# The first steps of a token-mixing kernel: plain products instead of a seven-product scheme, and an earlier start for the rows and weights that feed them

## The chip, the cores and the metric

The kernel runs on one core of one Trainium2 chip. The metric is the device time of one execution in microseconds (us). Three executions of the kernel before took 1442.42, 1442.47 and 1443.08 us; the median is 1442.47 us. Engines are named as in the profile: PE (matrix products), PEld (its weight loads), DVE (vector engine), ACT (scalar engine), POOL and SP (here they mostly issue DMAs). A PSUM tile is the accumulator that PE writes; DVE and ACT read it out.

## The reference

With B = 8 batches, S = 4224 tokens and D = 192 channels, cut to what matters:

```python
# lightweight convolution: 7 taps per head, causal, softmaxed weights
x = einsum('hk,bskhg->bshg', softmax(weight), windows(x))
# phase mixing
theta = x @ w_theta
zr, zi = x * cos(theta), x * sin(theta)
y = einsum('ts,bsd->btd', w_tok_r, zr) + einsum('ts,bsd->btd', w_tok_i, zi)
u = x + y
out = u + relu(u @ w_ch)
```

Nearly all of the arithmetic is the token mixing: two 4224 x 4224 matrices (real and imaginary) applied to 1536 columns (8 batches of 192 channels).

## The kernel before, in words

**Chunks and steps.** The 4224 source tokens are cut into 33 chunks of 128 (class `Chunk`), the 4224 target tokens into 33 blocks of 128, two blocks making a *unit*. At most NW = 11 chunks are held in SBUF. A `Step` mixes all chunks that are held with the weights of one unit and adds the result to the unit's partial rows `pv` (DRAM `part0`/`part1` between steps). In the first steps the chunks are still arriving: step 0 has n = 2 chunks, step 1 has 4, step 2 has 5, step 3 has 7, step 4 has 9, all later ones 11.

**A chunk's preparation** has this order: its rows are loaded by POOL (`xw`, L197) and the 16 rows ahead of them copied from the chunk before by SP (L188); `conv(0)` and `conv(1)` are 8 matmuls each into a PSUM tile `pc` (L210), read out into the chunk's tile `z` (L151 on ACT or L149 on DVE); 12 transposes into `tp` (L165), read out into `uT`; `theta(0)` and `theta(1)` are 8 matmuls each into `v` (L141, one for each half of the batches), each followed by two sines on ACT (L246: cosine and sine); then on DVE two products x·cos and x·sin (`product`, L251) and four differences T1, T2, T3, T4 (`sums`, L257). `pc`, `v` and `tp` share two PSUM buffers, so each of these PE groups also waits until the tile two places before it has been read out.

**A step's weights.** POOL loads the fp32 weights as 16-bit into a staging tile `st` (L323, two buffers, one for the real and one for the imaginary matrix of a step). DVE turns four blocks of them (`turn`, L336: "11" and "21" from the real one, "12" and "22" from the imaginary one) and forms four sums (`wsum`, L348: S1 to S4). A new `st` load can be issued only when the block turned last from the old one is done. POOL and SP issue in a fixed order, so what waits holds up all that stands behind it.

**A step's products** (`runs`, `mix`, L443). Seven products of a Strassen-like scheme stand for the eight that two target blocks (1, 2) and two matrices on two channel halves would need. Each product is a *run* over the step's n chunks (2 matmuls of 128 x 384 per chunk). Runs alternate between two or three PSUM accumulators, and an accumulator is given out to `pv` in the middle of its life and then accumulated further:

```python
("11", Z11, "c1", True, (0, 0, True)),
("S1", T1, "c2", True, (1, 1, True)),
("S2", T2, "c1", False, (0, 1, True)),
("S4", Z22, "c2", False, (0, 1, False)),
("S3", T3, "c1", False, (1, 1, False)),
("12", Z21, "c3", True, (0, 0, False)),
("22", T4, "c1", False, (1, 0, True)),
```

The last column is what is given at the end of the run: target block, channel half, and whether a first visit may copy. `give` (L400 to L408) copies with ACT (L406) where it may, and adds with DVE (L408) where not; in the steps of the first round a step has four copies and three adds. The next run on the same accumulator has to wait for the give. There are two PSUM buffers for accumulators (`ypool`), so the third accumulator "c3" also waits for the give of S4.

**What sets the order.** Every engine's order is the order in which the program is written (`in_order`). The front (L664 to L711) is a loop over i = 0 to 12 that prepares chunk i and finishes chunk i - 1, and calls `more(n)` between the pieces, which takes up to n matmul pairs from the stream of mixing as far as the chunks are ready (`ready[0]`); in the first turns it puts in dummy matmuls instead (`idle`, L590). Work of the next steps (turns, weight sums, loads of weights and rows, `step_events`) hangs on positions 0 to 7 inside a step.

Of the kernel before, what the change touches and what calls it, by code (L numbers as in the profile page):

```python
# [10 lines left out]
ALU = mybir.AluOpType  # L11
# [5 lines left out]
def kernel(  # L17
# [42 lines left out]
    NU = (NT + 1) // 2  # L60
    NW = 11
    PC = 512

    base = [0, 0, 1, 1, 2, 3, 3, 4, 4, 5, 5]
    assert len(base) == NW
# [65 lines left out]
    def token(k, a):  # L131

        return (a * NK + k) * Q
# [39 lines left out]
        )  # L173

    Z11, T1, Z21, Z22, T2, T4, T3 = range(7)

    class Chunk:

# [23 lines left out]
        def conv(self, j):  # L202

            if j == 0:
                self.z = zpool.tile([P, 7, HN], F16, name="z", tag="z")
                self.x = self.z[:, T2 : T2 + 2, :].rearrange("p t n -> p (t n)")
            pc = banks("pc")
            for h in range(4):
                for half in range(2):
                    pe(nc.tensor.matmul(  # L210
                        pc[half * 2 * Q : (half + 1) * 2 * Q, h // 2,
                           h % 2 * B * G : (h % 2 + 1) * B * G],
                        lhsT=bands[:, 4 * j + h, :, :].rearrange("p a m -> p (a m)"),
                        rhs=self.xw[:, half, :, (4 * j + h) * G : (4 * j + h + 1) * G],
                        start=True, stop=True,
                    ))
            evacuate(
                self.x.rearrange("p (b d) -> p b d", d=D)[
                    :, :, 4 * j * G : 4 * (j + 1) * G
                ].rearrange("p b (i h g) -> p i h b g", i=2, h=2),  # L220
                pc[:, :, 0 : 2 * B * G].rearrange("p i (h b g) -> p i h b g", h=2, b=B),
                self.k == 0 and j == 1,
            )
            if j == 1:
                for a in range(NQ):
                    t0 = token(self.k, a)
                    nc.sync.dma_start(
                        out=xs[t0 : t0 + Q, :], in_=self.x[a * Q : (a + 1) * Q, :]
                    )

        def transpose(self):
            self.xT = turned()
            transposed(self.xT, self.x, range(NG), self.k < 2)

        def theta(self, g):
            v = channel_mix(self.xT[:, 6 * g : 6 * g + 6, :], wth).rearrange(
                "p k (b h e) -> p k b h e", b=2, h=2
            )
            for first, bias in ((Z11, half_pi[:]), (Z21, None)):
                o = self.z[:, first : first + 2, :].rearrange(  # L240
                    "p h (k b e) -> p k b h e", b=2, e=HD
                )[:, 2 * g : 2 * g + 2, :, :, :]
                args = dict(out=o, in_=v, func=AT.Sin)
                if bias is not None:
                    args.update(bias=bias, scale=1.0)
                act(nc.scalar.activation(**args))  # L246

        def product(self, first):
            o = self.z[:, first : first + 2, :].rearrange("p h (b e) -> p h b e", e=HD)
            xv = self.x.rearrange("p (b h e) -> p h b e", h=2, e=HD)  # L250
            dve(nc.vector.tensor_tensor(out=o, in0=xv, in1=o, op=ALU.mult))  # L251

        def sums(self, which):
            z = self.z
            for o, a, b in (((T3, Z22, T1), (T1, T1, Z11)),
                            ((T2, Z22, T1), (T4, Z21, T2)))[which]:
                dve(nc.vector.tensor_tensor(  # L257
                    out=z[:, o, :], in0=z[:, a, :], in1=z[:, b, :], op=ALU.subtract
                ))

        def tasks(self):

# [22 lines left out]
    class Step:  # L285


        def __init__(self, t):
            self.t, self.u, self.ks = t, unit(t), active(t)
            self.n = len(self.ks)  # L290
            self.tbs = [tb for tb in (2 * self.u, 2 * self.u + 1) if tb < NT]
            self.pair = len(self.tbs) == 2
            self.first = t < NU
            self.final = t + NU >= NSTEP
            self.late = self.final and self.n < NW
            visits = [v for v in range(NU, NSTEP) if v % NU == t % NU]
            quiet = [v for v in visits if start[2 * NW - 1] < v <= 2 * NU]
            self.adds, self.ahead = [], []
            for i, tb in enumerate(self.tbs):
                known = self.known(tb)  # L300
                if t not in ([v for v in quiet if known < v - 1] or visits[-1:])[:1]:
                    continue
                if not self.late:
                    self.adds.append(i)
                else:
                    far = known <= start[2 * NW - 1]
                    self.ahead.append((i, 2 * NU - NW + 2 * (t % NU) if far else start[-1],
                                       (t // NU - 1 - far) % 2))
            self.time = 0.324 * self.n * (7 if self.pair else 4)
            self.st, self.w, self.xr, self.ub, self.uT, self.pv = {}, {}, {}, {}, {}, []  # L310

        def known(self, tb):
# [41 lines left out]
        def w_tasks(self):  # L354

            if not self.pair:
                return [(0.25, lambda: self.turn("11")), (4.2, lambda: self.turn("12"))]
            return [
                (0.25, lambda: self.turn("11")), (1.2, lambda: self.turn("21")),
                (2.05, lambda: self.wsum("S3")), (2.2, lambda: self.turn("22")),  # L360
                (3.05, lambda: self.wsum("S1")), (3.3, lambda: self.wsum("S2")),
                (4.2, lambda: self.turn("12")), (5.1, lambda: self.wsum("S4")),
            ]
# [46 lines left out]
        def runs(self):  # L410
# [16 lines left out]
                ("12", Z22, "c2", False, (0, 1, False)),  # L427
            ]

        def mix(self, events):  # L430

            runs = self.runs()
            events = sorted(events, key=lambda e: e[0])
            y = {}
            for r, (wn, zn, cn, opens, to) in enumerate(runs):
                if opens:
                    y[cn] = ypool.tile([P, 2, PC], F32, name="y", tag="y")
                for c, k in enumerate(self.ks):
                    while events and events[0][0] * len(runs) <= 7 * (r + c / self.n):
                        events.pop(0)[1]()  # L440
                    yield k
                    for q in range(2):
                        pe(nc.tensor.matmul(  # L443
                            y[cn][:, q, 0:BH],
                            lhsT=self.w[wn][:, c, :, :].rearrange("p bt i -> p (bt i)"),
                            rhs=chunks[k].z[:, zn, q * BH : (q + 1) * BH],
                            start=(opens and c == 0), stop=(c == self.n - 1),
                            skip_group_check=True,
                        ))
                if to:  # L450
                    self.give(y[cn], *to)
            for _, f in events:
# [52 lines left out]
            return found  # L505

    steps = [Step(t) for t in range(NSTEP)]
    outputs = [
        (sum(s.time for s in steps[: t + 1]) + at, f)
        for t in range(NSTEP) if steps[t].final for at, f in steps[t].outputs()  # L510
# [2 lines left out]
    def step_events(t):  # L513
# [11 lines left out]
        if t + 2 < NSTEP:  # L525
            nxt = steps[t + 2]
            for m in (1, 2):
                found.append((1.3 + 3 * (m - 1), lambda m=m: nxt.load_w(m)))
        if t == NU - 2:
            def load_wch():  # L530
                dve(nc.vector.memset(wch[:, 1:3, :], 0.0))
# [129 lines left out]
    load_chunk(3)  # L661
    for m in (1, 2):
        steps[1].load_w(m)
    for i in range(NW + 2):  # L664
        ch = chunks.get(i) if i < NW else None
        old = chunks[i - 1] if 0 < i <= NW else None

        def between(n):
            left = more(n)
            if 0 < i < 3:  # L670
                idle(min(left, 2))

        if ch:
            ch.conv(0)
        between(2)
        if old:
            old.theta(0)
        between(1)
        if ch:
            ch.conv(1)  # L680
        if i == 0:
            idle(4)
        ready[0] = i - 2
        between(2)
        if old:
            old.theta(1)
        if i == 1:
            for at, f in steps[0].w_tasks():
                if at < 2.2:
                    f()  # L690
        if i + 3 < NW:
            load_chunk(i + 3)
        between(1)
        if ch:
            ch.transpose()
        if old:
            old.product(Z11)
        between(2)
        if i == 1:
            for at, f in steps[0].w_tasks():  # L700
                if at >= 2.2:
                    f()
        if old:
            old.product(Z21)
        between(1)
        if old:
            old.sums(0)
        between(1)
        if old:
            old.sums(1)  # L710
        between(1)  # L711
    ready[0] = NK
# [33 lines left out]
```

## Time and profile before

| what | value |
|---|---|
| median of the three executions | 1442.47 us |
| the profiled execution | 1441.24 us |
| its span (first to last instruction) | 1439.4 us |
| PE busy in the span | 1410.6 us, 98% |
| DVE busy | 977.7 us, 68% |
| ACT busy | 316.0 us, 22% |
| POOL busy | 435.2 us, 30% |
| mean of the matmuls of the mixing (L443) | 326 ns from start to end, 7656 of them |

The times of a matmul overlap with the next one's, so a group is costed by starts: 47 matmuls of the mixing take 7.80 us from 92.52 us on, 0.166 us each. Busy shares are a mean over the span; the front has other limits than the rest, so it is read from the waits and the timeline of its own stretch. In rows of the timeline the first two numbers are start and duration, the brackets give the idle time of the engine before the row and what ended it.

### The profile page before, as it was taken

The page shows a single profiled execution, that of the slowest core. Times are in us where ns is not written, and L with a number is a line of the kernel's source. Part 1 is how long each engine was busy: PE and PEld are TensorE (multiplying, and loading weights), DVE is VectorE, ACT ScalarE, POOL GpSimd, SP SyncE. Part 2 cuts the span into 40 slices and gives each one's busy share as a digit, 9 for nine tenths or more (in the row PEclk, how much of TensorE's full clock was granted, in tenths as well). Part 3 has the DMA queues.
Part 4 walks back from the last instruction along what each step waited for, and adds up shares of the span by engine and source line. Part 5 has one row for each costly group of instructions (what it writes and reads, how often), then busy time and mean ns, then how long its engine had stood idle before and what let it go on. Part 6 is the DMA issues. An engine that isn't in the chain of part 4 may idle for free.

```text
span 1439.4 us, 23742 instructions
## 1 busy us (share of the span) xinstructions
PE 1410.6 (98%) x9809; PEld 890.2 (62%) x9809; DVE 977.7 (68%) x1050; ACT 316.0 (22%) x379; POOL 435.2 (30%) x655
## 2 busy tenths in 40 slices
PE   7899999999999999999999999999999999999997
PEld 4556666666666666666666666666566666666665
DVE  6893555545548787766666657877777677767686
ACT  6861101111125254000000004435200110010133
POOL 8421211111233232532433343233323123213120
PEclk9999999999999999999999999999999999999999
DMA  9976756465699999998899989989999999999884
GB/s 174 244 159 144 147 102 151 87 150 100 132 234 214 238 247 227 231 243 181 218 253 214 243 143 248 238 188 251 264 219 202 213 213 212 204 204 189 167 207 141
DMA packets 272028, 281.98 MB, mean 196 GB/s; under 512 B 106672, under 2 KB 240176, under 8 KB 271920
## 3 DMA queue, kind: packets, MB, share of 16 engines
q0 software_dynamic: 162464, 92.15, 48.8%
q1 hardware_dynamic: 71824, 178.88, 35.2%
q10 hardware_dynamic: 37632, 9.44, 4.6%
q8 instruction: 77, 1.26, 0.3%
q14 instruction: 31, 0.25, 0.1%
HBM read 245.49 MB, written 108.13 MB: 246 GB/s over the span
## 4 chain that ended last, share of the span: by engine, by line
PE 89%; DVE 4%; DMA 2%; ACT 2%; issue 1%; POOL 1%; DVEq 0%; SPq 0%; ACTq 0%
PE y L443 81%; PE v L141 5%; PE tp L165 1%; DMA xw<-in_x_dram 1%; PE pc L210 1%; ACT z L246 1%; DMA xw<-xw 1%; DVE pv L408 1%; DVE z L257 1%; DVE z L251 1%; DVE wt L336 1%; POOL st L323 0%; DVE pv L476 0%; ACT uT L151 0%; DVE wt L348 0%
## 5 line engine op out<-in xcount | busy, mean ns | idle before, releaser
L443 PE MATMUL y<-z,wt 128*128 128x384 f16 x7656 | 1279.6, 326 | 10.0 <-DVE pv L408 6.9
L443 PEld LDWEIGHTS <-wt 128*128 128x128 f16 x7656 | 742.5, 98 | 487.3 <-issue 9.8
L408 DVE TENSOR_TENSOR pv<-y,pv 128x768 f32<-128x768 f32 x324 | 309.1, 954 | 321.1 <-PE y L443 281.0
L336 DVE STREAM_TRANSPOSE wt<-st 128x1408 f16<-128x1408 f16 (+7 forms) x224 | 327.9, 1466 | 45.4 <-PE y L443 39.1
L323 POOL DMA_DIRECT2D st<-in_moe_w_tok_r_dram x232 | 132.7, 579 | 459.5 <-DVE wt L336 455.9
L323 POOL DMA_DIRECT2D st<-in_moe_w_tok_i_dram x232 | 132.7, 579 | 410.4 <-DVE wt L336 402.8
L348 DVE TENSOR_TENSOR wt<-wt 128x1408 f16<-128x1408 f16 (+7 forms) x216 | 174.4, 807 | 41.2 <-PE y L443 38.5
L151 ACT ACTIVATE z<-pc 128x768 f16<-128x768 f32 x65 | 50.9, 818 | 386.0 <-PE pc L210 383.3
L151 ACT ACTIVATE ub<-pv 128x768 f16<-128x768 f32 x63 | 50.3, 837 | 334.2 <-DVE pv L408 311.7
L406 ACT ACTIVATE pv<-y 128x768 f32<-128x768 f32 x66 | 54.1, 819 | 281.6 <-PE y L443 281.6
L141 PEld LDWEIGHTS <-uT 128*128 128x128 f16 x1056 | 91.2, 98 | 26.2 <-issue 7.8
L386 POOL TENSOR_TENSOR pv<-pv,xr 128x1536 f32<-128x1536 f32 x24 | 74.5, 3104 | 63.9 <-DVE pv L476 21.9
L197 POOL DMA_DIRECT2D xw<-in_x_dram x132 | 76.3, 585 | 28.2 <-DMA xw<-xw 8.3
L476 DVE SCALAR_TENSOR_TENSOR pv<-v,pv 128x768 f32<-128x768 f32 x66 | 62.9, 955 | 27.5 <-PE v L141 27.0
L257 DVE TENSOR_TENSOR z<-z 128x768 f16<-128x768 f16 x132 | 73.4, 556 | 3.6
L151 ACT ACTIVATE uT<-tp 128x1536 f16<-128x1536 f16 (+1 forms) x49 | 59.8, 1222 | 56.5 <-PE tp L165 56.5
L246 ACT ACTIVATE z<-v,half_pi 128x768 f16<-128x768 f32 x66 | 59.9, 908 | 55.0 <-PE v L141 54.4
L251 DVE TENSOR_TENSOR z<-z 128x1536 f16<-128x1536 f16 x66 | 60.0, 948 | 6.6 <-ACT z L246 6.6
L141 PE MATMUL v<-wth,uT 128*128 128x192 f16 x528 | 55.0, 248 | 4.8 <-ACT z L246 2.8
L141 PE MATMUL v<-wch,uT 128*128 128x192 f16 x528 | 54.2, 246 | 2.1 <-DVE pv L476 1.2
L246 ACT ACTIVATE z<-v 128x768 f16<-128x768 f32 x66 | 53.5, 811 | 0.0
L210 PE MATMUL pc<-xw,bands 96*64 96x192 f16 x528 | 31.4, 255 | 1.4 <-DVE bands L630 0.8
(43 smaller groups left out, 141.5 us busy)
## 6 DMA issues: line engine op xcount, KB each, us to landing
part<-pv SPq DMA_DIRECT2D x79, 768.0 KB, 4.2
pv<-part SPq DMA_DIRECT2D x79, 768.0 KB, 6.1
out_dram<-pv SPq DMA_DIRECT2D x66, 384.0 KB, 4.5
st<-in_moe_w_tok_r_dram POOLq DMA_DIRECT2D x136, 176.0 KB, 5.9
st<-in_moe_w_tok_i_dram POOLq DMA_DIRECT2D x136, 176.0 KB, 5.1
xs<-z SPq DMA_DIRECT2D x132, 96.0 KB, 4.9
xw<-in_x_dram POOLq DMA_DIRECT2D x121, 96.0 KB, 5.5
xr<-xs SPq DMA_DIRECT2D x24, 384.0 KB, 4.6
```

Of the source, the lines that this page charges most:

```text
L141: pe(nc.tensor.matmul(v[:, k, b * D : (b + 1) * D], lhsT=tT[:, 3 * k + b + i, :], rhs=w[:, 2 * b + i, :], start=(i == 0), stop=(i == 1),))
L151: act(nc.scalar.activation(out=out, in_=in_, func=AT.Copy))
L197: nc.gpsimd.dma_start(out=self.xw[lo : lo + n, h, :, :], in_=x[:, t0 : t0 + n, :].rearrange("b s d -> s b d"),)
L246: act(nc.scalar.activation(**args))
L251: dve(nc.vector.tensor_tensor(out=o, in0=xv, in1=o, op=ALU.mult))
L257: dve(nc.vector.tensor_tensor(out=z[:, o, :], in0=z[:, a, :], in1=z[:, b, :], op=ALU.subtract))
L323: pool(nc.gpsimd.dma_start(out=st[a * Q : (a + 1) * Q, 0:nb, :, 0:n] .rearrange("i r bt s -> i (r bt) s"), in_=w[self.tbs[0] * P : (self.t ...
L336: dve(nc.vector.transpose(self.w[name][:, 0 : self.n, :, :], self.st[int(name[1])][:, int(name[0]) - 1, :, 0 : self.n * Q] .rearrange("p b ...
L348: dve(nc.vector.tensor_tensor(out=self.w[name][:, 0 : self.n, :, :], in0=self.w[a][:, 0 : self.n, :, :], in1=self.w[b][:, 0 : self.n, :, : ...
L386: ins = pool(nc.gpsimd.tensor_tensor(out=self.pv[i], in0=self.pv[i], in1=self.xr[i], op=ALU.add))
L408: dve(nc.vector.tensor_tensor(out=o, in0=yv, in1=o, op=ALU.add))
L443: pe(nc.tensor.matmul(y[cn][:, q, 0:BH], lhsT=self.w[wn][:, c, :, :].rearrange("p bt i -> p (bt i)"), rhs=chunks[k].z[:, zn, q * BH : (q + ...
```

## The change

- **Plain products.** Where a step of the first round has a pair of target blocks and at most NP = 4 chunks (steps 0 and 1, `plain`), it mixes the eight plain products: four blocks of weights, each with two channel halves, no S and no T operands. Each of the four results is given once, by a copy. The first target block is mixed chunk by chunk, the second one half after the other.
- **Order of the slots.** The second half of x·cos (Z12) is now made in the slot of T3 (`raw`), so that T1 is a new tile and T3 is formed in place. Chunks 0 to 3 need no T operands until step 2; their T1, T2, T4 are formed during step 1 and their T3 during step 2 (`step_events`).
- **Chunk 0 in batch halves.** Its convolution, transposes and products are each made in two halves of four batches (`conv_batches`, `transpose_batches`, `product` with `gs`). It has 32 convolution matmuls of 96 columns instead of 16 of 192.
- **Who reads PSUM out.** DVE instead of ACT takes the transposes of chunks 2 and 3, both convolution halves of chunk 1 and the second ones of chunks 2 and 3; chunk 0 is shared.
- **Rows and turns.** The loads of chunks 4 and 5 are written ahead of the loop. The turns of steps 0 and 1 are written into turns i = 1 and i = 3 of the loop. `ready[0]` is raised one piece sooner. The dummy matmuls fall from 33 to 21.

The built order shows what of this the engines see. On POOL the loads of chunks 4 and 5 stand where they stood, behind both weight loads of step 1; the first weight load of step 3 now stands ahead of chunk 8 instead of behind it. On SP the store of step 0's first `pv` block now stands ahead of the halo copies of chunk 5 instead of behind those of chunk 6. From step 4 on all engines have the order that they had.

```diff
+    NP = 4
+    Z12 = T3
@@ conv
-                self.k == 0 and j == 1,
+                self.k == 1 or (self.k in (2, 3) and j == 1),
@@
+        def conv_batches(self, g):
...
+            for h in range(H):
+                for half in range(2):
+                    pe(nc.tensor.matmul(
+                        pc[half * 2 * Q : (half + 1) * 2 * Q, h // 4,
+                           h % 4 * GB * G : (h % 4 + 1) * GB * G],
+                        lhsT=bands[:, h, :, :].rearrange("p a m -> p (a m)"),
+                        rhs=self.xw[:, half, g * GB : (g + 1) * GB, h * G : (h + 1) * G],
+                        start=True, stop=True,
+                    ))
+            for i in range(2):
+                evacuate(
...
+                    i == 1,
+                )
+        def raw(self, first):
+            return self.z[:, 0:7:6, :] if first == Z11 else self.z[:, Z21 : Z21 + 2, :]
@@ transpose
-            transposed(self.xT, self.x, range(NG), self.k < 2)
+            transposed(self.xT, self.x, range(NG), self.k < 4)
+        def transpose_batches(self, g):
+            if g == 0:
+                self.xT = turned()
+            transposed(self.xT, self.x, [g], True)
@@ sums
-            for o, a, b in (((T3, Z22, T1), (T1, T1, Z11)),
+            for o, a, b in (((T1, Z12, Z11), (T3, Z22, Z12)),
@@ Step
-            self.time = 0.324 * self.n * (7 if self.pair else 4)
+            self.plain = self.first and self.pair and self.n <= NP
+            self.time = 0.324 * self.n * (8 if self.plain else 7 if self.pair else 4)
@@ w_tasks
+            if self.plain:
+                return []
@@
+        def products(self):
...
+            for i, name in enumerate(("c1", "c2")):
+                a, b = f"{i + 1}1", f"{i + 1}2"
+                cells = [
+                    (r, c, h) + w for c in range(self.n) for h in range(2)
+                    for r, w in enumerate(((a, (Z11, Z12)[h]), (b, (Z21, Z22)[h])))
+                ]
+                if i:
+                    cells.sort(key=lambda e: (e[2], e[0]))
+                for r, c, h, wn, zn in cells:
+                    done = r == 1 and c == self.n - 1
+                    yield (wn, zn, f"c{h + 1}", c, r == 0 and c == 0, done,
+                           (i, h, True) if done else None)
@@ step_events
+        if t in (NPS, NPS + 1):
+            for j, k in enumerate(k for k in range(NK) if start[k] <= NPS):
+                for o, a, b, at in (
+                    ((T1, Z12, Z11, 0), (T2, Z22, T1, 0.3), (T4, Z21, T2, 0.6)),
+                    ((T3, Z22, Z12, 0),),
+                )[t - NPS]:
+                    found.append((
+                        (1.3 + 1.4 * j if t == NPS else 1.2 + 0.6 * j) + at,
+                        lambda k=k, o=o, a=a, b=b: chunks[k].sum(o, a, b),
+                    ))
@@ the loop of the front
-    for i in range(NW + 2):
+    load_chunk(4)
+    load_chunk(5)
+    for g in range(NG):
+        chunks[0].conv_batches(g)
+    idle(2)
+    for g in range(NG):
+        chunks[0].transpose_batches(g)
+    for i in range(1, NW + 2):
...
-            if 0 < i < 3:
-                idle(min(left, 2))
+            if i < 3:
+                idle(min(left, 2) if i == 1 else 0)
...
-        if i == 1:
-            for at, f in steps[0].w_tasks():
-                if at < 2.2:
-                    f()
+        if i in (1, 3):
+            for name in ("11", "21"):
+                steps[i // 2].turn(name)
...
+        if i in (1, 3):
+            for name in ("12", "22"):
+                steps[i // 2].turn(name)
...
-        if old:
+        if old and start[i - 1] > NPS:
             old.sums(0)
```

## The prediction

> **What bounds the kernel now.** I read four views, from coarse to fine. The page says that PE is busy 98% of the span; after about 104 us it hardly waits at all, so whatever the change does lies ahead of that, and the time moves with the moment from which PE runs without waits. The waits of PE in the first 100 us name what holds it there:
>
> ```profile
> PE y L443 <- ACT pv L406: 3.0, 3, 1.2
> PE v L141 <- ACT z L246: 2.8, 7, 0.7
> PE y L443 <- DVE pv L408: 2.7, 4, 1.0
> ```
>
> The gives of step 0 (L406, L408) cost about as much as the sines. The timeline of PE shows where:
>
> ```profile
> 33.53 0.81 PE L443 MATMUL y<-z,wt 128*128 128x384 f16 x4 [1.13 <-ACT pv L406]
> 35.57 0.48 PE L443 MATMUL y<-z,wt 128*128 128x384 f16 x2 [1.23 <-ACT pv L406]
> ...
> 37.72 0.82 PE L443 MATMUL y<-z,wt 128*128 128x384 f16 x2 [0.78 <-DVE pv L408]
> 38.33 1.49 PE L141 MATMUL v<-wth,uT 128*128 128x192 f16 x8
> ```
>
> With two chunks a run of step 0 is 4 matmuls, 0.7 us; a give takes 0.8 to 0.95 us, so runs wait for gives, and theta of chunk 3 stands behind them. It also runs in 1.49 us instead of 0.82 us, at a granted clock of 0.71 between 36 and 40 us. Then the timeline of DVE:
>
> ```profile
> 43.68 1.83 DVE L251 TENSOR_TENSOR z<-z 128x1536 f16<-128x1536 f16 x2 [1.48 <-ACT z L246]
> ...
> 50.45 1.83 DVE L251 TENSOR_TENSOR z<-z 128x1536 f16<-128x1536 f16 x2 [1.81 <-ACT z L246]
> ...
> 58.93 0.84 DVE L336 STREAM_TRANSPOSE wt<-st 128x640 f16<-128x640 f16 x1 [1.41 <-PE y L443]
> ...
> 81.34 1.11 DVE L336 STREAM_TRANSPOSE wt<-st 128x896 f16<-128x896 f16 x1 [1.43 <-PE y L443]
> ...
> 102.76 0.95 DVE L408 TENSOR_TENSOR pv<-y,pv 128x768 f32<-128x768 f32 x1
> ```
>
> From chunk 3's first product (43.68) to the add of step 3's run S4 (102.76, ends 103.71) DVE idles 1.81 + 1.41 + 1.43 = 4.65 us of 60.0. Last the chain of waits: from 82.38 us it lies on DVE (products, differences, adds) until
>
> ```profile
> 102.84 0.88 DVE pv L408
> 103.77 6.35 PE y L443 x38
> ```
>
> where PE, which stood for 2.31 us, takes run "12" and never waits long again. So **the time moves with the moment at which DVE ends this add**.
>
> **Step 1: until chunk 3's sines end.** In the built order I lay the instructions end to end with the durations of the rows. Equal until 9.94 us.
> - Chunk 0: 32 convolution matmuls for 16 (1.43 us). A matmul of half the columns is not in the trace; its weight load is (0.072 us), the whole one took 0.089, so 2.3 to 2.85 us, I take 2.6. Its four half readouts at 0.5 and its half transposes follow one another, two dummies go. First theta at 15.4 instead of 15.08: 0.3 us lost; if half a matmul costs half, 0.6 gained.
> - Chunk 1: dummies ahead of it go, theta at 20.8 instead of 21.04.
> - Chunk 2: its transposes are read out by DVE (0.96, end 26.05) instead of ACT (1.45, end 27.35), theta at 26.2 instead of 27.41. DVE is free for it: its turns shrink by the four sums of 0.29.
> - Chunk 3: transposes 29.7; before, uT waited behind two sines and a copy on ACT and began at 33.32; on DVE 30.55 to 31.45. A plain step has no give inside; the fifth matmul pair of block 2 waits only for the second copy (31.8). Convolution of chunk 4 at 32.2 (35.99), theta at 33.3 (38.33) at the full clock, second theta 35.8 (41.83), sines end 38.6. Before, 43.52 + 0.83 = 44.35.
>
> So chunk 3's first product could begin at 38.6 instead of 43.68: **5.1 us**. Chunk 4's rows hide behind this: POOL issues them from 24.75 (25.12 before), since it still waits for step 0's turns; at the row's 4.8 us to landing they are there at 31.9, 0.3 us ahead of need. "Sooner" is worth nothing here, and each us of lateness would cost one.
>
> **Step 2: DVE from there to the add.** Costed by starts: a difference 0.555 (four in 2.22), an add 0.93. In this stretch before, 32 differences and 7 adds. After: chunks 0 to 3 bring T1, T2, T4, T3 here, 44 in all, +12 x 0.555 = 6.7; three adds of step 1 are gone, -2.8. Products (16), turns and weight sums of steps 2 to 4 stay. Work +3.9: 55.4 + 3.9 = 59.3 us. The idle 4.65 us go: two of its gaps were waits for sines, and ACT now runs ahead (its period was 50.97 - 44.21 = 6.8 us per chunk, DVE's work is 59.3 / 8 = 7.4); the other two were turns that waited for a weight tile, and a plain step uses four of the nine tiles instead of eight. **Net gain of the stretch 0.75 us.**
>
> New idle time: the first turn of step 2 stands ahead of chunk 3's product and waits for its weights. POOL issues them when step 1's turns end (30.15) and chunk 4's rows land, 30.4 to 32.7; at 5.0 us they land at 37.7, the turn (0.84) ends at 38.5. That cover is gone if they are later, and two stores of 768 KB from step 0 now leave SP at about 32 and 36.5 instead of 44.45. What lies beside such stores is in the list of DMA issues, for the issues from 44.3 to 47 us (times to landing last):
>
> ```profile
> part<-pv SPq DMA_DIRECT2D x2, 768.0 KB, 7.4
> xw<-in_x_dram POOLq DMA_DIRECT2D x4, 96.0 KB, 9.3
> ```
>
> 9.3 instead of about 4.8. Weights beside a store: 5.0 to 9.3. I take 1.0 us late, nearer to 5.0, since one store, not two, lies beside them. Plus 0.4 us for chunk 10: PE's run "12" of step 2 needs the add of that step's S4. Up to its end DVE has 36.6 us of rows from 38.6, so about 76 with the lateness; PE is there at about 72 and stands some 4 us, and chunks 9 and 10 follow that.
>
> **Step 3: PE and the rest.** Plain products add (4 + 8) matmuls x 0.166 = 2.0 us; 12 dummies go. Neither is on the path: PE would be at run "12" of step 3 by 94.5 (from chunk 4's uT to chunk 10's last theta 44.21 to 92.52 before, so 38.6 + 48.3 = 86.9; then 46 matmuls x 0.166 = 7.6), DVE's add ends at 38.6 + 59.3 + 1.4 = 99.3. From there the order is the same. Sum: -5.1 - 0.75 + 1.0 + 0.4 = **-4.4 us**: 1441.24 becomes 1436.8; for the median of the runs 1442.47 - 4.4 = 1438.1.
>
> The clock: 0.71 was granted after gaps of only 1.13, 1.23 and 0.78 us. The Trainium skill, "TensorE: Matmul & The Clock Gate", Part 1, halves the clock after an idle window of some 3.4 us. No gap here was that long, so the row decides that short gaps do it too; by the page the new stand of 4 us ahead of "12" would halve the clock for up to 3.4 us, an estimate of 1.7 us on PE, of which some 1 us would reach chunk 10's sines and the add. That speaks against the change; by it the sum would be -3.4.
>
> **Rivals.**
> 1. *Loads late, gain eaten.* Step 2's real weights land after 9.3 us, at 42.0; the turn ends at 42.8, chunk 3's product begins 4.2 us later than it could: 4.2 replaces 1.0, gain 1.2, 1441.3. For it: DMA engines are over 90% busy from 4 to 40 us. Against: step 2's weights took 5.0 before.
> 2. *Loads late twice, slower.* The real weights take 10.5 us (the longest of a row load in this trace) and land at 43.2; the imaginary ones are issued only after that load's first parts, at about 41 to 43, and take as long, to 53.7, where DVE wants them at 48.6. That idles DVE 5.4 + 5.1 us, so -5.1 - 0.75 + 10.5 + 0.4 = +5.1: 1447.6. It decides from a sum of 8.3 us of lateness on.
> 3. *DVE is no bound.* If differences and products hide better than by their rows, PE goes on at 94.5 to 95.5 instead of 103.77: 8.3 us less at the later end, 1434.2. Against: the chain lies on DVE already, and its work grows.
> 4. *The first part doesn't come.* Chunk 0 in halves and the rows' place are as good as neutral above; if the gives were not the cause, chunk 3 would stay at 44.35 and only the added 3.9 us against 4.65 would be left: 1441.7. The three named waits speak against it.
>
> **Chances.** Forecast (gain 2.5 to 6.5) 0.62; rival 1: 0.15; rival 2: 0.08; rival 3: 0.08; rival 4: 0.07. Range 1434.0 to 1443.5: it takes in rivals 1, 3 and 4 and leaves rival 2 out. What the measurement can tell from no change is about 0.2%, 2.9 us: faster 0.63 (rival 3 and all of the forecast but 0.07), same 0.29, slower 0.08.
>
> **What would show it.** Right: no wait for L406 or for an add in the first 40 us; chunk 3's first product at 38.5 to 40; DVE without idle gaps from there; PE waiting for the add of S4 in step 2 (3 to 4 us, near 72) and again ahead of "12" in step 3, going on at 99 to 100. Wrong: a turn of 640 columns that waits for a DMA for more than 2 us (rivals 1, 2); DVE gaps of over 2 us in all after 45; PE waiting for rows; or a granted clock under 0.9 for long in the front.

## The result and the profile after

The changed kernel takes 1437.35 us (median of 16 runs, 1435.46 to 1441.31) against 1441.68 us for the kernel before (16 runs, 1439.83 to 1449.47): 4.3 us less, a ratio of 0.9969 with a 95% interval of 0.9960 to 0.9977. Forecast were 4.4 us less. The profiled execution took 1437.24 us with a span of 1435.4 us, 4.0 us under that of before. The page's busy times, then the head of its chain:

```profile
PE 1410.6 (98%) x9825; PEld 890.3 (62%) x9825; DVE 973.8 (68%) x1046; ACT 310.8 (22%) x374; POOL 434.4 (30%) x655
...
PE 90%; DMA 5%; DVE 2%; ACT 1%; POOL 1%; issue 1%; DVEq 0%; ACTq 0%; POOLq 0%; SPq 0%
```

PE is as busy as before; its share of the chain rose from 89% to 90%, DVE's fell from 4% to 2%, and DMA's rose from 2% to 5%. That last pair tells what took over. PE's waits in the first 100 us:

```profile
PE pc L212 <- DMA xw<-xw: 3.3, 3, 1.6
...
PE y L513 <- ACT pv L454: 1.0, 2, 0.7
```

The waits for gives, 3.0 us on ACT and 2.7 us on DVE before, have shrunk to 1.0 us. New is 3.3 us of waiting for halo copies (L190). The timeline of PE has the theta of chunk 3, the new stall and the end of the stretch:

```profile
33.22 0.82 PE L142 MATMUL v<-wth,uT 128*128 128x192 f16 x8
...
71.59 0.24 PE L212 MATMUL pc<-xw,bands 96*64 96x192 f16 x1 [1.61 <-DMA xw<-xw]
72.79 0.82 PE L212 MATMUL pc<-xw,bands 96*64 96x192 f16 x7 [0.96 <-DMA xw<-xw]
...
100.93 7.33 PE L513 MATMUL y<-z,wt 128*128 128x384 f16 x44 [1.83 <-DVE pv L456]
```

Theta of chunk 3 runs 5.1 us sooner, at the full clock (0.82 instead of 1.49 us); run "12" of step 3 goes on at 100.93 instead of 103.77. DVE over the same stretch:

```profile
39.87 0.84 DVE L382 STREAM_TRANSPOSE wt<-st 128x640 f16<-128x640 f16 x1 [5.63 <-DMA st<-in_moe_w_tok_r_dram]
40.64 1.78 DVE L293 TENSOR_TENSOR z<-z 128x1536 f16<-128x1536 f16 x2
...
47.25 0.84 DVE L382 STREAM_TRANSPOSE wt<-st 128x640 f16<-128x640 f16 x1 [2.04 <-DMA st<-in_moe_w_tok_i_dram]
...
87.09 1.83 DVE L293 TENSOR_TENSOR z<-z 128x1536 f16<-128x1536 f16 x2 [1.20 <-ACT z L287]
...
99.92 0.95 DVE L456 TENSOR_TENSOR pv<-y,pv 128x768 f32<-128x768 f32 x1
```

Chunk 3's sines end at 37.74 + 0.84 = 38.58, and yet its product begins at 40.64, because the turn ahead of it waits for step 2's weights. The second load costs 2.04 us, chunk 9's sines 1.20 us. Where these come from is in the chain of waits:

```profile
58.06 1.10 POOL xw L199 x2
59.18 8.02 DMA xw<-in_x_dram
67.32 5.33 DMA xw<-xw
72.79 0.82 PE pc L212 x7
```

Chunk 9's rows take 8.0 us and its halo copy is issued behind SP's two stores of step 1 (768 KB each, issued from 58.30); PE gets it at 72.8, and what follows runs at half speed: the granted clock from 72.6 to 76.0 is 0.50. So theta of chunk 9 and its sines are late.

**Where the 4.0 us of span lie.** I take one turn of DVE, the one that starts at 205.75 us in the changed kernel, as a mark; counted from the end it is the same instruction in every kernel here, and from well ahead of it on PE, DVE and ACT have the same order. Before reaches it at 208.59: 2.84 us lie ahead of the mark, the other 1.1 us behind it, in code that the change doesn't touch. How far that second part differs from one execution to another, the column "rest" of the table below shows.

### The profile page after: what moved, and what is told of

The parts are those of the page before. It is cut to its first block, busy times and chain, and to the rows that moved or that the text cites. A ratio compares the mean times of both kernels' runs of the same rounds, so it can differ in the third digit from the quotient of the medians.

```text
span 1435.4 us, 23761 instructions
## 1 busy us (share of the span) xinstructions
PE 1410.6 (98%) x9825; PEld 890.3 (62%) x9825; DVE 973.8 (68%) x1046; ACT 310.8 (22%) x374; POOL 434.4 (30%) x655
## 4 chain that ended last, share of the span: by engine, by line
PE 90%; DMA 5%; DVE 2%; ACT 1%; POOL 1%; issue 1%; DVEq 0%; ACTq 0%; POOLq 0%; SPq 0%
PE y L513 81%; PE v L142 5%; DMA xw<-in_x_dram 2%; DMA st<-in_moe_w_tok_r_dram 2%; PE tp L166 1%; PE pc L212 1%; ACT z L287 1%; DVE wt L382 1%; POOL st L369 1%; DVE pv L456 1%; DVE pv L546 0%; POOL xw L199 0%; DMA xw<-xw 0%; DMA st<-in_moe_w_tok_i_dram 0%; DMA wsb<-in_weight_dram 0%
## 5 line engine op out<-in xcount | busy, mean ns | idle before, releaser
L456 DVE TENSOR_TENSOR pv<-y,pv 128x768 f32<-128x768 f32 x318 | 303.3, 954 | 321.4 <-PE y L513 281.3
L382 DVE STREAM_TRANSPOSE wt<-st 128x1408 f16<-128x1408 f16 (+7 forms) x224 | 327.4, 1465 | 50.1 <-PE y L513 36.2
L394 DVE TENSOR_TENSOR wt<-wt 128x1408 f16<-128x1408 f16 (+6 forms) x208 | 173.3, 833 | 40.2 <-PE y L513 38.0
L152 ACT ACTIVATE z<-pc 128x768 f16<-128x768 f32 (+1 forms) x62 | 47.5, 803 | 385.6 <-PE pc L212 381.3
L152 ACT ACTIVATE uT<-tp 128x1536 f16<-128x1536 f16 (+1 forms) x47 | 56.7, 1209 | 56.9 <-PE tp L166 56.9
L293 DVE TENSOR_TENSOR z<-z 128x1536 f16<-128x1536 f16 (+1 forms) x68 | 60.6, 926 | 4.2 <-ACT z L287 4.2
```

Of the source, the lines that this page charges most:

```text
L152: act(nc.scalar.activation(out=out, in_=in_, func=AT.Copy))
L382: dve(nc.vector.transpose(self.w[name][:, 0 : self.n, :, :], self.st[int(name[1])][:, int(name[0]) - 1, :, 0 : self.n * Q] .rearrange("p b ...
L394: dve(nc.vector.tensor_tensor(out=self.w[name][:, 0 : self.n, :, :], in0=self.w[a][:, 0 : self.n, :, :], in1=self.w[b][:, 0 : self.n, :, : ...
L456: dve(nc.vector.tensor_tensor(out=o, in0=yv, in1=o, op=ALU.add))
```

## The experiments

My theory was that plain products let chunk 3 finish sooner, and that from there DVE, fed by the weight loads, sets the moment at which PE runs free. Rivals: the readouts that moved to DVE, or chunk 0's halves, make the gain; PE is the bound; the loads set it all. Each kernel ran 10 to 12 times. "Ratio" is to runs of the kernel before, taken beside it. The table is worked out from the traces: the first convolution matmul, the mark at 205.75 us less that start (the front), the span behind the mark (the rest), and the start of the add behind S4 of step 3, counted from the start of the span, so that the five kernels with a first convolution at 8.9 us have 1.1 us of advance in it. A trace shows one execution, which took up to 3.8 us more (e1) or 2.5 us less (e2) than the median of its kernel, so front and rest do not add up to the median.

```
kernel                first conv   front   rest    S4 add   median   ratio (95%)
before                    9.94    198.65  1230.8   102.76   1441.68  1
changed                   9.96    195.79  1229.7    99.92   1437.35  0.9969 (0.9960-0.9977)
e1 no plain products      9.94    201.78  1233.7   105.90   1443.30  1.0010 (0.9997-1.0024)
e2 plain products alone   9.97    197.86  1229.3   102.00   1441.32  0.9991 (0.9980-1.0002)
e3 old readouts           8.86    197.46  1230.9   100.49   1437.10  0.9968 (0.9957-0.9979)
e4 chunk 0 whole          8.85    196.12  1235.5    99.14   1439.47  0.9981 (0.9970-0.9992)
e5 rows late              9.97    198.13  1231.1   102.28   1441.06  0.9995 (0.9985-1.0005)
e6 late stores            9.97    193.82  1230.1    97.96   1437.92  0.9973 (0.9960-0.9986)
e7 more on DVE            8.86    201.87  1230.5   103.22   1441.71  0.9993 (0.9982-1.0004)
e8 less on DVE            9.97    196.96  1230.2   101.10   1437.86  0.9977 (0.9967-0.9987)
e9 paced rows             9.93    194.62  1235.8    98.73   1440.43  0.9991 (0.9968-1.0015)
e10 plain and rows        8.89    199.53  1229.6   102.60   1442.00  1.0006 (0.9995-1.0018)
e11 rows alone            8.86    198.41  1230.8   101.45   1441.39  0.9999 (0.9990-1.0007)
e12 stores late, paced    9.94    193.80  1238.1    97.92   1441.28  1.0000 (0.9991-1.0010)
```

### Without plain products

```diff
-    NP = 4
+    NP = 0
...
-        if i in (1, 3):
-            for name in ("11", "21"):
-                steps[i // 2].turn(name)
+        if i == 1:
+            for at, f in steps[0].w_tasks():
```

> The changed kernel with steps 0 and 1 mixed by seven products and weight sums again; chunk 0's halves, the readouts on VectorE and the early rows stay. Theory (the plain products let chunk 3 be ready sooner, because VectorE and ScalarE no longer make differences, weight sums and copies for steps 0 and 1 between the chunks): the gain is lost, chunk 3's first product at 43 us or later, time 1440.5 to 1443. Rival A (the readouts that moved to VectorE make the gain by themselves): chunk 3's first product near 41, time 1437 to 1438.5.

Measured 1443.30 us: the whole gain is gone (whether it is slower than before, the interval of 0.9997 to 1.0024 leaves open). Chunk 3's sines end at 47.92. Rival A falls: the rest of the change without plain products gains nothing. What is back is PE's wait for adds, in its waits between 20 and 120 us:

```profile
PE y L513 <- DVE pv L456: 7.4, 5, 2.1
```

In the same view PE waits 2.8 us, once, for DVE's readout of a convolution: loaded with differences, weight sums and adds, DVE is late with the readouts that were moved to it. So these readouts bring nothing on a DVE that still has that work.

### Plain products alone

```diff
-                self.k == 1 or (self.k in (2, 3) and j == 1),
+                self.k == 0 and j == 1,
...
-            transposed(self.xT, self.x, range(NG), self.k < 4)
+            transposed(self.xT, self.x, range(NG), self.k < 2)
...
-    load_chunk(4)
-    load_chunk(5)
-    for g in range(NG):
-        chunks[0].conv_batches(g)
+    for j in range(2):
+        chunks[0].conv(j)
...
-        ready[0] = i - 2
         between(1)
         if ch:
             ch.conv(1)
+        ready[0] = i - 2
```

> The kernel before with the plain products alone (with the second step's turns and the differences where the change has them); chunk 0 whole, readouts split as before, rows of chunks 4 and 5 in their old place. Theory: chunk 3's sines end at 41 to 42 us, because ScalarE still has its old readouts, its first product follows at 42 to 43, and a part of the gain comes: 1438.5 to 1440.5. Rival A (readouts make the gain): 1441 to 1443. Rival B (plain products are all of it): 1437 to 1438.

Measured 1441.32 us, which can't be told from before; I had expected more of it. Chunk 3's sines end at 40.37, even sooner than the 41 to 42 expected, but chunk 4's at 50.1 and chunk 5's at 59.0 (46.5 and 54.8 in the changed kernel), and DVE waits 11.8 us for sines in all. So plain products are needed and are not enough: the sooner sines of chunk 3 are given back at chunks 4 and 5.

### Old readouts, and chunk 0 whole

```diff
-                self.k == 1 or (self.k in (2, 3) and j == 1),
+                self.k == 0 and j == 1,
...
-            transposed(self.xT, self.x, range(NG), self.k < 4)
+            transposed(self.xT, self.x, range(NG), self.k < 2)
```

> The changed kernel with the readouts of chunks 1 to 3 split between ScalarE and VectorE as before. Theory: chunk 3's sines end 2 to 3 us later than 38.6, at 41 to 41.5, and its first product at 41.5 instead of 40.64, since the turn that waits for the second step's weights hides the first 2 us: time 0.5 to 1.5 above the changed kernel, 1438 to 1439. Rival A (readouts make the gain): 1440.5 to 1442. Rival C (the weight loads set it all): under 0.3 more, 1437.4.

Measured 1437.10 us, level with the changed kernel: rival C. From the first convolution to the end of chunk 3's sines it takes 29.57 instead of 28.62 us, so the readouts do cost 0.95 us. At chunk 3's product nothing of it is left (30.7 us behind the first convolution in both), because the turn ahead of it waits longer than that:

```profile
38.75 0.85 DVE L382 STREAM_TRANSPOSE wt<-st 128x640 f16<-128x640 f16 x1 [5.78 <-DMA st<-in_moe_w_tok_r_dram]
```

The front of this execution is nevertheless 1.67 us longer than the changed kernel's: chunk 9's convolution waits 1.81 + 1.22 us for DMAs here, and its product comes 1.7 us later, counted from the first convolution. In the median that doesn't show, so what the readouts are worth stays open within these 1.7 us.

The other one makes chunk 0 whole:

```diff
-    for g in range(NG):
-        chunks[0].conv_batches(g)
-    idle(2)
-    for g in range(NG):
-        chunks[0].transpose_batches(g)
+    for j in range(2):
+        chunks[0].conv(j)
+    idle(4)
+    chunks[0].transpose()
```

> The changed kernel with chunk 0's convolution, transposes and products whole again. Theory: the first theta comes 0.3 us later (15.1), chunk 3's sines 0.3 later (38.9), and nothing of it is left at chunk 3's first product, which waits for the turn of the weights at 39.87: time 1437.2 to 1437.8. Rival D (the start of the chain of chunks carries through to the end): 0.3 to 0.9 more, 1437.7 to 1438.3, first product of chunk 3 at 41 or later.

Measured 1439.47 us, 2.1 us more than the changed kernel, which neither case gave. Its front is only 0.3 us longer, the expected amount. What its profiled execution loses, it loses far behind, in the rest (1235.5 instead of 1229.7), and that execution took 1442.33 us, 2.9 more than its kernel's median. The two intervals overlap (0.9970 to 0.9992 and 0.9960 to 0.9977), so whether the halves are worth 0.3 or 2 us stays open.

### Rows of chunks 4 and 5 in their old place

```diff
-    load_chunk(4)
-    load_chunk(5)
```

> The changed kernel with the rows of chunks 4 and 5 loaded in their old place, inside the loop; all else as changed. The prediction's step gave the earlier rows nothing: 1437.4, within 0.5 of the changed kernel. Rival E, formed from the run of the plain products alone, where chunk 5's sines ended at 59.0 instead of 54.8: the early rows are a part of the gain; VectorE waits for the sines of chunks 4 and 5, the add behind S4 of step 3 comes at 101 to 102 instead of 99.9, time 1438.5 to 1440.

Measured 1441.06 us: rival E, and 3.7 us where the prediction's step had put nothing. The timelines of POOL, DVE and PE of this kernel:

```profile
30.40 2.28 POOL L369 DMA_DIRECT2D st<-in_moe_w_tok_r_dram  x4 [3.61 <-DVE wt L382]
32.67 3.46 POOL L199 DMA_DIRECT2D xw<-in_x_dram  x6
...
39.14 2.36 POOL L369 DMA_DIRECT2D st<-in_moe_w_tok_i_dram  x4
```

```profile
49.77 0.85 DVE L382 STREAM_TRANSPOSE wt<-st 128x640 f16<-128x640 f16 x1 [6.30 <-DMA st<-in_moe_w_tok_i_dram]
```

```profile
41.95 0.49 PE L212 MATMUL pc<-xw,bands 96*64 96x192 f16 x7 [1.71 <-DMA xw<-xw]
43.52 1.49 PE L142 MATMUL v<-wth,uT 128*128 128x192 f16 x8
```

In this order chunk 5's rows stand behind step 2's real weights, and the imaginary weights behind eight row loads instead of four. They land so late that DVE stands for 6.30 us, and chunk 5's convolution waits for its halo, after which theta of chunk 4 (which stands behind it on PE) runs at half clock. In the kernel before, both chunks' rows stood ahead of step 2's weights without this edit: it is the other parts of the change that would move them back, and the two lines keep them where they were.

The next two kernels were meant to find the least that makes the gain: the same two lines, on top of plain products alone (e10) and on top of the kernel before (e11).

```diff
         steps[1].load_w(m)
+    load_chunk(4)
+    load_chunk(5)
```

> The kernel before with two parts of the change alone: the plain products, and the rows of chunks 4 and 5 loaded ahead. Readouts and chunk 0 as before. Theory (these two make the gain, and only together: the runs with either one missing stood at 1441 and 1443): the add behind S4 of step 3 at 99.5 to 101, time 1437 to 1438.5. Rival J (chunk 0 in halves carries 2 us of it, as the run with chunk 0 whole could be read): 1439 to 1440.5.

> The kernel before with the rows of chunks 4 and 5 loaded ahead and nothing else. Theory (VectorE's work of steps 0 and 1 stands between the chunks there, so that rows which land sooner find it busy): no gain, 1441 to 1443, chunk 3's first product at 43 or later. Rival K (the early rows make the gain by themselves): 1437.5 to 1439.

Measured 1442.00 and 1441.39 us. In these two kernels the edit moves nothing but one chunk's halo copies, ahead of two row stores on SP; POOL, PE, DVE and ACT keep the order of the kernels that they start from. So they test less than I had written down: they are almost repeats of plain products alone (1441.32) and of before, and say how far a repeat lies off, 0.7 us or less in the median and 1.7 us in the front of a single profile (199.53 and 197.86). The theory of the first expectation falls: plain products with the rows in good order aren't enough. Which of the rest (chunk 0's halves, the readouts, the earlier `ready` with its other interleaving of mixing) they lack was not taken apart; by the run with old readouts it isn't the readouts alone.

### Is DVE the bound?

```diff
-                    ((T1, Z12, Z11, 0), (T2, Z22, T1, 0.3), (T4, Z21, T2, 0.6)),
+                    ((T1, Z12, Z11, 0), (T2, Z22, T1, 0.3), (T4, Z21, T2, 0.6),
+                     (T4, Z21, T2, 0.7)),
```

> The changed kernel with the difference T4 of chunks 0 to 3 computed twice inside step 1: four more differences of 0.55 us, 2.2 us more work for VectorE, same results. Theory (from chunk 3's first product to the add behind S4 of step 3 VectorE is the bound): that add comes 1.5 to 2.2 us later, at 101.4 to 102.1, and the time is 1.5 to 2.2 more, 1438.9 to 1439.6. Rival H (loads or TensorE set that stretch): 0 to 0.5 more.

```diff
-                    ((T3, Z22, Z12, 0),),
+                    (),
```

> The changed kernel without the difference T3 of chunks 0 to 3: four differences of 0.55 us less for VectorE inside step 2 (the product with S3 then reads the raw plane that stands in its place; this leaves a part of the computation out). If VectorE alone is the bound of the stretch: the add behind S4 of step 3 comes 2.2 us sooner, 97.7, and the time is 1435.2. Theory (VectorE and the sines of chunk 9 are nearly tied there, VectorE waited 1.20 us for them): 0.3 to 1.5 us sooner, 1436 to 1437. Rival H (loads or TensorE set it): no difference.

More work cost 3.5 us by the ratios and 4.4 by the medians (1441.71), well over the 2.2 us that I had added; less work gained nothing that the runs can tell (1437.86; the 1435.2 of a DVE that alone is the bound lies outside the interval). So DVE has no slack, but it isn't the last to finish. With less work it stands for 2.87 us ahead of an add of step 2, and then waits for chunk 9 all the same:

```profile
88.27 1.83 DVE L293 TENSOR_TENSOR z<-z 128x1536 f16<-128x1536 f16 x2 [1.27 <-ACT z L287]
...
101.10 0.95 DVE L456 TENSOR_TENSOR pv<-y,pv 128x768 f32<-128x768 f32 x1
```

From chunk 9's product to the add are 12.83 us here, and 12.82 to 12.84 in the changed kernel, e3, e4, e5, e6, e9 and e12: the whole tail hangs on this product. Chunk 9's convolution waited 2.16 + 0.92 us for halo copies in this execution. With more work the add comes 4.4 us later, counted from the first convolution. Of that 2.1 us are there before any of the added work: DVE stands 7.72 us ahead of the first turn, for its load. From chunk 3's product to the add it takes 61.58 us instead of 59.28, 2.3 us more, as much as was added. On the way PE stands 4.03 us at "12" of step 2, where the forecast had put such a wait, with a half clock behind it. So about half of what this profile loses is not the added work.

### Partial sums stored later

```diff
+    PUT = (4, 2)
...
-            if not self.final:
-                for i, tb in enumerate(self.tbs):
-                    nc.sync.dma_start(...)
+            if not self.final and self.t >= 2:
+                self.put()
...
+            if t in (1, 2):
+                found.append((PUT[t - 1], steps[t - 1].put))
```

> The changed kernel with the stores of the partial sums of steps 0 and 1 held until four sevenths of step 1 and two sevenths of step 2 (behind the halo copies of chunks 7 and 9). Theory (the second step's weight loads come late because they run beside these stores): the loads land some 5 us after their issue, the turn that waited until 39.87 starts at 37.5 to 38.5, the second wait of 2.04 goes, chunk 9's convolution waits under 0.5 for its halo, the add behind S4 of step 3 comes at 97.5 to 99; time 1434.5 to 1436.5. Rival F (the DMA engines are full in this stretch whatever the order): the turn stays at 39 to 40, time 1437 to 1438. Rival G (the late stores hold the z slots that chunks 7 to 10 need): slower, 1439 or more.

In the front the theory holds point by point:

```profile
36.38 0.84 DVE L383 STREAM_TRANSPOSE wt<-st 128x640 f16<-128x640 f16 x1 [2.56 <-DMA st<-in_moe_w_tok_r_dram]
37.49 1.83 DVE L294 TENSOR_TENSOR z<-z 128x1536 f16<-128x1536 f16 x2 [0.26 <-ACT z L288]
...
85.13 1.83 DVE L294 TENSOR_TENSOR z<-z 128x1536 f16<-128x1536 f16 x2 [0.16 <-ACT z L288]
...
97.96 0.95 DVE L457 TENSOR_TENSOR pv<-y,pv 128x768 f32<-128x768 f32 x1
```

The turn starts at 36.38 instead of 39.87, the product follows the sines, chunk 9 waits 0.16 instead of 1.20 us, no half clock is left in the front, and the add comes 2.0 us sooner. The twelfth kernel, with the same front, repeats it (97.92). The profiled execution took 1435.72 us, 1.5 less than the changed kernel's, and was the second fastest of its twelve. And still the median of 12 runs is 1437.92 us, no better. Since only one run has a trace, where the others lost it isn't seen. That an earlier add makes an earlier end is thus shown in traces, but not in the median of this kernel.

### What makes runs of one kernel differ

The column "first conv" shows one source. Up to it all fourteen kernels have the same code, but the 32 small matmuls ahead of it take 2.64 us in some executions and 1.57 us in others; first the changed kernel, then e4:

```profile
6.54 2.64 PE L705 MATMUL bp<-taps,sel 7*96 7x8 f16 x32 [1.39 <-DVE taps L701]
```

```profile
6.50 1.57 PE L705 MATMUL bp<-taps,sel 7*96 7x8 f16 x32 [1.35 <-DVE taps L701]
```

That puts the first convolution at 9.95 or 8.86 us whatever was changed. It is the clock: in the five executions with 1.57 us (e3, e4, e7, e10, e11) the clock records of the traces show the full clock from 5.2 to 5.6 us on, for 3.41 us, and in the nine with 2.64 us not before 13.4 us. The other source lies in the rest, near 1016 us; again the changed kernel, then e4 with its chain of waits:

```profile
1016.58 1.65 DVE L382 STREAM_TRANSPOSE wt<-st 128x1408 f16<-128x1408 f16 x1 [1.67 <-DMA st<-in_moe_w_tok_r_dram]
```

```profile
1020.15 1.65 DVE L382 STREAM_TRANSPOSE wt<-st 128x1408 f16<-128x1408 f16 x1 [3.87 <-DMA st<-in_moe_w_tok_r_dram]
```

```profile
1000.04 19.98 DMA st<-in_moe_w_tok_r_dram
```

In e4 a weight load of 176 KB a piece is on its way for 20 us, while five loads of partial sums (768 KB each) are issued between 998 and 1006 us (997 to 1003 in the changed kernel). In e4 PE then waits 2.62 us and drops to half clock for 3.4 us. I tried to take that away by holding those loads back, everywhere (e9) or there alone, on top of the late stores (e12):

```diff
                     ins = nc.sync.dma_start(
                         out=pv, in_=part[(self.t // NU - 1) % 2][tb, :, :]
                     )
+                    tc.add_manual_dep(ins.ins, last["dve"].ins.name, SYNC, reason="pace")
```

> The changed kernel with the loads of the partial sums (768 KB each) held to the place in the order where they are written, so that five of them no longer start together near 1000 us. Of six traces with the same order there, the weight load issued at 997 to 1003 us landed 15 to 20 us later and the stretch from step 3's end to 1105 us behind it took 895.7 to 901.6 us. Theory (this load's landing is what makes runs of one kernel differ by several us): VectorE's wait for it (1.67 to 3.87) goes under 0.5, time 1435 to 1436.7, and its runs spread less than the 5.9 us of the changed kernel's. Rival I (the spread has another source, the loads are late anyway): 1437 to 1438, same spread.

> The late stores of the sixth experiment, and the loads of the partial sums held to their place for steps 38 to 42 alone, where three to five of them start together near 1000 us. Theory (two things on top of the change: the front's loads come sooner by 1 to 2 us, and the late weight load near 1000 us no longer lands 15 to 20 us after its issue): the add behind S4 of step 3 at 97.5 to 98.7, VectorE's wait near 1016 under 0.5, time 1434 to 1436.3. Rival I (the spread of the runs has another source): 1437 to 1438.

Both failed: 1440.43 and 1441.28 us, and the runs of e9 spread more, not less (1435.07 to 1456.24). In each the wait near 1016 is gone and a larger one stands elsewhere. In e9 an add makes PE stand for 3.68 us at 604 us; in e12, behind a transfer that turns the output rows:

```profile
1052.71 1.46 PE L143 MATMUL v<-wch,uT 128*128 128x192 f16 x8 [5.79 <-DMA uT<-ub]
```

From the turn near 1016 to another near 1101 us e12 takes 94.9 us, the changed kernel 84.8. So the theory that this load makes the spread is neither shown nor refuted: what I moved came back as another wait. None of the twelve is faster than the changed kernel by more than the runs differ.

## Why the prediction was right, point by point

- **Step 1, chunk 3's sines at 38.6 instead of 44.35: right.** 38.58 measured, the transposes of chunk 3 at 29.46 (29.7), its theta at 33.22 (33.3). The cause holds too: with plain products alone the sines end at 40.37, which is 4.0 of the 5.8 us, and without them at 47.92. Chunk 0 in halves came out on the good side: 32 matmuls of 96 columns take 1.42 us (9.96 to 11.38), as 16 of 192 took 1.43, so theta comes 0.3 us sooner, not later. One reading was too broad: of the 5.7 us of waits for gives in the first 100 us only 1.13 + 1.23 + 0.78 = 3.1 us are step 0's, the others come from 53 us on.
- **"Sooner" is worth nothing for the rows: wrong.** I weighed chunk 4's rows alone and against the kernel before. What counts is the order that the rest of the change would give without the two lines: chunk 5's rows behind step 2's weights, and the imaginary weights behind four more row loads. That costs 3.7 us in the median.
- **1.0 us late for step 2's weights: too small.** Chunk 3's product began 2.06 us after the sines (at 40.64 instead of 39.6), and the imaginary ones cost 2.04 us more, for which the sum had nothing. The reason given, the stores beside them, is right: with late stores the turn starts 3.5 us sooner.
- **DVE's work +3.9: too large, and that hid the former.** DVE is busy for 55.93 us from chunk 3's product to the end of the add (40.64 to 100.87), against 53.95 us before (43.68 to 103.71): 2.0 us more. The count was right (44 differences, 4 adds), but five differences in a row cost 2.59 us, from 52.05 to the turn at 54.64, which is 0.52 each and not 0.555. The 55.4 from which I started was the time less the named waits, and so had 1.4 us of short gaps in it that no row names. The idle time did not go: 2.04 + 1.20 + 0.27 = 3.51 us of named waits stand where 4.65 stood, and the stretch takes 60.23 us instead of 60.03, not 0.75 less.
- **The stand of PE ahead of "12" of step 2, 0.4 us: didn't come.** PE itself was late, by chunk 9's halo copy (1.61 + 0.96 us) and the half clock behind it. Nothing in the sum had put that in. It is this that sets chunk 9's product and with it the add. Where chunk 9's halo came in time, PE did stand there, for 1.46 us (e6) and 1.48 us (e12).
- **The add ends at 99.3: 100.87.** In the terms of the sum the profile has -5.1 for the sines (as forecast), +2.1 for the late weights instead of +1.0, and +0.2 for the stretch to the add instead of -0.75 + 0.4: together -2.8 instead of -4.4. e9, whose order in the front is the changed kernel's, ended the add at 99.68, so a single profile is good to about 1.2 us here. The front, to which the whole sum belongs, thus gives 2.8 us of gain in one profile and 4.0 in the other; the rest of the 4.3 us lies in code that is the same, where executions differ by several us. So the first and largest term was right, and that the total agrees to 0.1 us is luck.
- **The signs.** Of the signs of being right, the waits for gives in the first 40 us are gone, and PE does stand ahead of "12" of step 3 (until 100.93, not 99 to 100). Of the signs of being wrong three came all the same: turns of 640 columns that waited 5.63 and 2.04 us for a DMA, 3.51 us of gaps on DVE behind 45 us, and PE waiting for rows and halos.
- **"DVE sets the moment": half right.** More work on it costs time, less gains none. The product of chunk 9 sets it, and in the changed kernel that is set by a DMA; from there to the add it is DVE's work all the same.
- **The clock.** Of the Trainium skill, "TensorE: Matmul & The Clock Gate", Part 1, I had set the idle window of 3.4 us against gaps of about 1 us. The runs side with the gaps, but not with every gap: 1.61 + 0.96 us in the changed kernel and 1.71 us in e5 are followed by a half-clock stretch, while 1.83 us ahead of "12" of step 3 in the changed kernel, 2.31 us there in the kernel before, and 2.09 us at 39.7 us in e9 are not. The clock records of the traces show what tells them apart. In every trace the clock changes only on a grid of 3.413 us. I add up PE's idle time in each stretch of the grid that has the full clock: 1.95 us or more was always followed by a half-clock stretch, under 1.58 us never, and between them both occur. The two gaps of the changed kernel fall into one stretch (2.41 us idle, up to 72.63 us), and the gap of 1.83 us is cut into 0.83 and 1.00. The length agrees with the page's window of 3413 ns: the half clock lasts 3.41 us, or twice that behind 5.79 us of waiting in e12, 2.16 + 0.92 us in e8 and 2.80 us in e1.

## What to carry to other kernels

When a change moves work forward, go through each queue that its DMAs stand in, not for where a load is written but for what it ends up behind; here two lines that seem to move nothing are worth 3.7 us, and a store that moved sooner cost the loads beside it 2 us and a halo copy 2.6 us. Look for the one event from which the tail has a fixed length (12.83 us here, in eight kernels): what makes that event sooner brings the tail forward, and work taken off an engine that still waits ahead of it need not. Where single profiles differ by 1 to 2 us in code that is the same, a sum that hits the total may have got there by luck: check it term by term.

## What the runs showed of the hardware

- Half a matmul costs half at the start: 32 of 64 x 96 columns in 1.42 us, 16 of 64 x 192 in 1.43 us. Both ran ahead of the first full-clock stretch, where four dummies of 384 columns take 1.46 us (four matmuls of the mixing take 0.82 us later on); at the full clock no run shows it.
- The clock halves for 3.41 us where PE was idle for about half of the 3.413 us stretch before, in one gap or in several (1.59 to 1.93 us: sometimes; 1.95 us or more: always, in fourteen traces). So a gap can cost more than its length, and the same gap costs nothing more where the grid cuts it in two.
- DVE reads transposes (128 x 1536) out of PSUM in 0.96 us, where ACT took 1.45 us.
- Step 2's real weights (80 KB a piece) took 7.6 us to land beside a store of 768 KB, and 4.6 us where the store was held back (e6). Beside five loads of 768 KB the pieces of 176 KB took 12.0 us in the median in the changed kernel, and the last of them 20 us in e4.
